# A new order for a fused sparse-attention and quick-GELU kernel: which engine adds, masks and copies from the tenth ff tile on

## The chip, the cores and the metric

The kernel runs on one core of a Trainium2 chip. Its time is the device time of one execution in microseconds; several runs are taken and their median is compared. The engines of the core are TensorE (PE in the profile, its weight loads PEld), VectorE (DVE), ScalarE (ACT), GpSimd (POOL) and SyncE (SP); transfers are issued from the queues of POOL and SP.

## What is computed

The reference first computes attention, then a feed-forward layer on its output:

```python
def _attn_ref(q, k, v):                      # (4, 8, 768, 64) each
    k_sum = k.reshape(B, H, nb, block, D).max(axis=3)      # block 32
    v_sum = v.reshape(B, H, nb, block, D).mean(axis=3)
    scores_l = scale * np.matmul(q, k.transpose(0, 1, 3, 2))
    mask_l = np.abs(pos[:, None] - pos[None, :]) < window  # window 16
    scores_s = scale * np.einsum('bhsd,bhnd->bhsn', q, k_sum) + np.log(block)
    a = softmax(concatenate([where(mask_l, scores_l, -1e9), scores_s]))
    return np.matmul(a, np.concatenate([v, v_sum], axis=2))

def _moe_ref(x, w_in, w_out):                # x (3072, 512), w_in (512, 2048)
    h = x @ w_in
    g = h * (1.0 / (1.0 + np.exp(-1.702 * h)))
    return g @ w_out                         # (3072, 512)
```

Each query thus sees 31 near keys and 24 block sums.

## The kernel before

The work runs batch by batch (0 to 3), and within a batch in three parts that are interleaved with those of the next batch. **Attention**: keys and queries of a batch are loaded by `pool.dma_start` (tiles `kb`, `qb`; values `vw`), turned (`kx`, `qT`; for batches 2 and 3 by transposing transfers on SP's queue), scored on TensorE in 64-row tiles (`ps_s`), exponentiated on ScalarE (`a_sb`), multiplied with a 0/1 mask `mk`, and multiplied with the values (`ps_av`). **ff**: `x @ w_in` for 16 tiles of 128 hidden units and two halves of 384 tokens, into PSUM tile `ph`; each tile is 4 matmuls of 128x384, and ScalarE writes its GELU to `gT`. **Products**: `g @ w_out` in a scheme with 7 instead of 8 block products (a Strassen-Winograd step), which needs sums and differences of quarters of `gT` (tile `gs`) and of `w_out` (tile `ws`); three groups of 128 tokens have seven products each (8 matmuls of 128x256 into `poA`, `poB`, `poC`), which are copied or added out of PSUM (`s`, `osb`) and stored.

Nothing is scheduled at run time: every instruction stands in a table of words, `ORDER`, that is played from the first to the last, and each engine runs its instructions in that order:

```python
    engines = {"d": dve, "a": act, "g": pool}
    for word in ORDER.split():
        name, *args = word.split(".")
        ops[name](*[engines[a] if a in engines else ... for a in args])
```

An engine therefore never passes an instruction that waits. The words that the change and the prediction speak of:

- `f.half.tile.k0123.bank`: one ff tile; `g.half.tile`: its GELU (ACT).
- `gs.j.n.what.engine`: one quarter sum over `n` hidden tiles (128x768 for n = 2, 128x384 for n = 1), VectorE if no engine is named. Sum 0 is the right half's two quarters added, 1 is sum 0 less a left quarter, 2 a difference of left and right, 3 the last one less sum 1.
- `p.t.what.bank`: product `what` of token group `t`; product 5 needs sums 0, product 6 sums 1, product 7 sums 2, product 3 sums 3, of all eight hidden tiles. `x.t.what.engine`: its copy or addition out of PSUM; `o`: the store.
- `s.b.half.pair.bank`, `e`, `m`, `v`, `nn`: scores, exponentials, mask product, values and normalisation. `vm` and `vb`: block sums of values.
- `lk`, `lq`, `lv`: loads on POOL's queue. `xk`, `xq`: transposing transfers on SP's queue. `xa`: block maxima of the transposed keys (DVE, `ka`); `ka`: copies of halo columns within `kx`; `kR`: the maxima written into `kx`; scores of the batch need all of these.
- `sd`, `ha`: small transfers within `vw` on SP's queue.

The helper that records every instruction is line 28, so all groups of the profile carry L28.

Of the kernel before, what the change touches and what calls it, by code (L numbers as in the profile page):

```python
# [49 lines left out]
f.1.0.k01.2 f.1.8.k23 ha.1.3.0 f.1.9.k0123.0 f.1.0.k23 ws.1.1 g.1.8 g.1.9 f.1.1.k0123.1 ws.2.0 f.1.2.k0123.3 g.1.0  # L50
f.1.3.k0123.2 g.1.1 ws.1.0 gs.0.2.0 ha.1.2.0 f.1.10.k0123.1 g.1.3 gs.0.2.1 f.1.4.k0123.2 g.1.2 gs.2.2.2 g.1.10 lv.1.5.0
gs.0.2.3 f.1.11.k0123.1 g.1.4 f.1.12.k0123.3 g.1.11 f.1.13.k0123.0 ws.3.1 tk.0.52 g.1.13 gs.2.2.0 g.1.12 kc.0.a
f.1.6.k0123.2 gs.0.2.2 gs.2.2.1 f.1.15.k0123.0 f.1.5.k0123.1 ws.3.0 g.1.6 g.1.5 tk.1.52 kc.1.a tk.2.42 kh.0.1.d ws.2.1
f.1.14.k0123.3 f.1.7.k0123.1 tk.3.52 gs.2.2.3 kc.2.a xm.0.1 tq.0.42 gs.4.2.0 g.1.15 kc.3.d p.0.2.0 g.1.7 g.1.14 gs.6.1.0
p.0.1.2 qc.0.a xm.1.1 tq.1.52 ha.1.1.0 gs.4.2.2 lq.2.0 x.0.1.a gs.4.2.1 gs.6.1.2 lq.2.2 gs.6.1.1 gs.7.1.0 ha.1.0.0
qc.1.a gs.6.1.3 lv.2.0.0 tq.2.42 p.1.1.3 qc.2.a gs.7.1.1 gs.4.2.3 p.0.5.1 x.0.5.a p.0.6 tq.3.52 kr.0.1.d s.1.0.0.42
x.0.6.a x.0.2.a gs.7.1.2 X gs.7.1.3 kr.1.1.d x.1.1.d xm.3.1 kh.2.1.g p.1.2.0 e.0.0 p.0.3 p.0.7 lq.2.3 m.0.0 x.0.3.a
x.0.7.a kh.1.1.d qc.3.d s.1.1.0.42 e.1.0 p.1.6 xm.2.1 vm.1.42 o.0.0.0.0.2 s.1.0.1.52 lv.2.5.0 e.0.1 kr.2.1.g kh.3.1.d
p.0.4 vb sd.1.1.0 x.0.4.a gate.1 s.1.1.1.52 e.1.1 lv.2.3.0 p.1.5.1 kr.3.1.d x.1.5.d x.1.2.a m.1.0 x.1.6.a s.1.0.2.52
# [904 lines left out]
```

## Time and profile before

| what | value |
| --- | --- |
| median of 3 runs | 212.17 us (210.46 to 212.53) |
| the profiled execution | 211.7 us, of which the span of the core is 210.0 us |
| mean granted clock of TensorE | 0.996 |
| busy: PE, DVE, ACT, POOL | 200.4, 130.8, 114.3, 109.1 us |
| instructions: DVE, ACT, POOL | 311, 227, 157 |
| loaded and stored | 27.26 MB read, 6.29 MB written |

The times of an engine are sums of its instructions' durations; an instruction that has begun but is held up counts as busy. Idle time of an engine that nothing waits for costs nothing, so the table says which engine is full, and not yet which wait is paid for.

### The profile page before, as it was taken

To read this page: it belongs to the slowest core of one execution; us is meant where nothing else is said; L and a number is where in the kernel's file an instruction comes from. 1 tells how busy PE (TensorE), PEld (TensorE's weight loads), DVE (VectorE), ACT (ScalarE), POOL (GpSimd) and SP (SyncE) were. 2 spreads that over 40 slices of the span, in tenths; PEclk is the share of its full clock that TensorE was granted. 3 is DMA by queue.
4 is the path that set the end of the run, shared out by engine and by line. 5 is a ranking of instruction groups with operands and counts; after the bars stand their busy time and mean duration, and the time that the engine had idled before them with its cause. 6 is when DMAs were issued, how large, how long until landed. Compare 5 with 4: busy or idle time off the path is not lost.

```text
span 210.0 us, 5880 instructions
## 1 busy us (share of the span) xinstructions
PE 200.4 (95%) x2440; PEld 145.8 (69%) x2440; DVE 130.8 (62%) x311; ACT 114.3 (54%) x227; POOL 109.1 (52%) x157
## 2 busy tenths in 40 slices
PE   7998798999999999999999999999999999999993
PEld 5656554667887886556788865657888865668882
DVE  5577873798997871168997822694888500166342
ACT  2473885659666736676764336567670157671100
POOL 7999972399982998448949422431000000863000
PEclk9999999999999999999999999999999999999998
DMA  4999999999999999999999999939215920000214
GB/s 67 162 166 189 209 213 221 182 144 122 99 134 199 156 177 183 130 126 141 148 166 204 142 227 180 187 29 169 50 53 139 160 105 0 0 3 0 100 53 150
DMA packets 96458, 27.74 MB, mean 132 GB/s; under 512 B 85024, under 2 KB 93488, under 8 KB 96432
## 3 DMA queue, kind: packets, MB, share of 16 engines
q0 software_dynamic: 70800, 13.64, 82.7%
q1 hardware_dynamic: 25632, 13.74, 33.2%
q8 instruction: 19, 0.31, 0.6%
q14 instruction: 7, 0.06, 0.1%
HBM read 27.26 MB, written 6.29 MB: 160 GB/s over the span
## 4 chain that ended last, share of the span: by engine, by line
PE 79%; POOL 12%; DMA 5%; issue 1%; DVE 1%; SPq 0%; POOLq 0%; DVEq 0%
PE ph L28 36%; PE poA L28 19%; PE poB L28 10%; PE poC L28 5%; PE ps_s L28 3%; PE ps_av L28 3%; DMA vw<-vw 2%; POOL mk L28 2%; DMA out_dram<-osb 2%; POOL v0n L28 2%; POOL w_in_sb L28 2%; POOL kb L28 2%; POOL kx L28 2%; POOL qb L28 1%; PE ps_t L28 1%
## 5 line engine op out<-in xcount | busy, mean ns | idle before, releaser
L28 PE MATMUL ph<-xT,w_in_sb 128*128 128x384 f16 x512 | 86.1, 326 | 0.4 <-DVE osb L28 0.4
L28 ACT ACTIVATE gT<-ph 128x384 f16<-128x384 f32 x128 | 56.1, 495 | 30.6 <-PE ph L28 29.9
L28 PEld LDWEIGHTS <-w_in_sb 128*128 128x128 f16 x512 | 49.2, 98 | 32.4 <-issue 0.9
L28 PEld LDWEIGHTS <-gs 128*128 128x128 f16 x384 | 36.5, 98 | 4.6
L28 DVE TENSOR_TENSOR gs<-gT 128x768 f16<-128x768 f16 (+1 forms) x36 | 17.5, 498 | 29.1 <-ACT gT L28 29.0
L28 POOL TENSOR_TENSOR gs<-gs,gT 128x768 f16<-128x768 f16 (+1 forms) x6 | 8.8, 1461 | 41.8 <-PE ph L28 32.7
L28 POOL DMA_DIRECT2D kb<-in_k_dram x28 | 23.1, 842 | 13.7 <-DMA w_out_sb<-in_moe_w_out_dram 6.4
L28 ACT ACTIVATE a_sb<-ps_s 128x768 bf16<-128x768 f32 x32 | 24.8, 808 | 9.5 <-PE ps_s L28 9.3
L28 PEld LDWEIGHTS <-gT 128*128 128x128 f16 x288 | 27.3, 98 | 3.6
L28 POOL DMA_DIRECT2D vw<-in_v_dram x36 | 25.7, 752 | 5.0 <-DMA w_out_sb<-in_moe_w_out_dram 1.7
L28 PE MATMUL poA<-ws,gs 128*128 128x256 f16 x192 | 24.8, 273 | 0.0
L28 POOL DMA_DIRECT2D qb<-in_q_dram x28 | 23.8, 867 | 1.8 <-issue 0.9
L28 DVE TENSOR_TENSOR a_sb<-a_sb,mk 128x768 bf16<-128x768 bf16 x28 | 14.7, 550 | 3.0 <-ACT a_sb L28 2.2
L28 DVE TENSOR_TENSOR x<-ps_av,rc 128x768 f16<-128x768 f32 (+1 forms) x18 | 15.6, 869 | 0.6
L28 ACT ACTIVATE s<-poA 128x256 f32<-128x256 f32 x14 | 5.4, 382 | 19.3 <-PE poA L28 18.6
L28 PE MATMUL poB<-ws,gs 128*128 128x256 f16 x96 | 12.5, 273 | 0.0
L28 PE MATMUL poC<-w_out_sb,gT 128*128 128x256 f16 x96 | 12.5, 273 | 0.0
L28 PE MATMUL poA<-w_out_sb,gT 128*128 128x256 f16 x96 | 12.4, 273 | 0.0
L28 PE MATMUL poB<-w_out_sb,gs 128*128 128x256 f16 x96 | 12.4, 273 | 0.0
L28 PE MATMUL poA<-ws,gT 128*128 128x256 f16 x96 | 12.3, 273 | 0.0
L28 DVE TENSOR_REDUCE ka<-kx 128x48 bf16<-128x1536 bf16 x4 | 7.0, 1750 | 7.4 <-DMA kx<-kb 7.4
...
(102 smaller groups left out, 219.0 us busy)
## 6 DMA issues: line engine op xcount, KB each, us to landing
...
```

The lines of the kernel that those rows point to most:

```text
L28: r = f(*a, **kw)
```

## The change

The first 180 words of `ORDER` stay. From there on, from the tenth ff tile of batch 0, all 822 words stand in another order; they are the same operations, and 46 of them name another engine:

- 10 more quarter sums are on GpSimd (21 where there were 11), and 5 mask products of the 32 are, where there was none.
- The halo copies `ka` of batch 2 go from GpSimd to VectorE, those of batch 3 from VectorE to GpSimd; one small `kr` copy goes to GpSimd.
- Copies out of PSUM are exchanged between VectorE and ScalarE, so that VectorE has 7 fewer and ScalarE 6 more instructions.

Two functions take the engine as an argument:

```diff
@@ ORDER, from word 181 on
-lk.1.5 lk.1.6 lq.1.2 lk.1.7 m.1.1 lq.1.1 lv.1.0.0 lq.1.4 lq.1.5 lq.1.7 lv.1.3.1 lq.1.6 lv.1.0.1 lv.1.2.0 lv.1.1.0 cv.1
+lk.1.5 lk.1.6 lq.1.2 lk.1.7 m.1.1 lq.1.1 lv.1.0.0 lq.1.4 cv.1 lq.1.5 lq.1.7 lv.1.3.1 f.0.8.k0123.2 lq.1.6 lv.1.0.1
...
@@ mask
-    def mask(half, p):
+    def mask(half, p, eng=dve):
         a = a_sb[half, p]
-        dve.tensor_mul(a, a, mk[:, half * TH:(half + 1) * TH, :].unsqueeze(1)
+        eng.tensor_mul(a, a, mk[:, half * TH:(half + 1) * TH, :].unsqueeze(1)
                        .to_broadcast([128, 2, TH, QT]))
@@ w_sum
-    def w_sum(what, part):
+    def w_sum(what, part, eng=dve):
...
-        dve.tensor_tensor(out=ws[:, what, c], in0=a, in1=b, op=ALU.subtract)
+        eng.tensor_tensor(out=ws[:, what, c], in0=a, in1=b, op=ALU.subtract)
```

No `ws` word names an engine, so those sums stay on VectorE.

Three places show what the table does to the queues. The first is GpSimd's queue in the ff part of batch 1. Before (`qb`, `kb` and `vw` are loads for the next batches, `kx` the halo copies):

```order
L28 DMA vw_106<-in_v_dram 64x8x64 x2
L28 DMA qb<-in_q_dram 128x6x64
L28 DMA vw_106<-in_v_dram 64x8x64
L28 DMA qb<-in_q_dram 128x6x64 x2
L28 DMA vw_107<-in_v_dram 64x8x64
L28 DMA kb<-in_k_dram 128x6x64
L28 TENSOR_TENSOR gs<-gs,gT 128x768
L28 DMA kb<-in_k_dram 128x6x64
L28 DMA vw_107<-in_v_dram 64x8x64
L28 COPY kx_102<-kx_102 128x4x5x16 x2
L28 COPY kx_102<-kx_102 128x24x2x16
```

and changed:

```order
L28 DMA vw_106<-in_v_dram 64x8x64
L28 TENSOR_TENSOR gs<-gT 128x768
L28 TENSOR_TENSOR gs<-gs,gT 128x768
L28 DMA qb<-in_q_dram 128x6x64
L28 TENSOR_TENSOR gs<-gs,gT 128x768
L28 DMA qb<-in_q_dram 128x6x64
L28 TENSOR_TENSOR gs<-gT,gs 128x768
L28 DMA vw_107<-in_v_dram 64x8x64
L28 DMA kb<-in_k_dram 128x6x64 x2
L28 TENSOR_TENSOR gs<-gT 128x384
```

The last two loads of queries of batch 2 (`lq.2.5`, `lq.2.7`) now stand behind two and three quarter sums, and the halo copies have left this queue for VectorE's.

The second is the same queue in batch 2, from the last loads of batch 3 on. Before:

```order
L28 DMA kb<-in_k_dram 128x6x64
L28 CAST gate_120<-xT_115 128x1
L28 DMA qb<-in_q_dram 128x6x64
L28 DMA vw_107<-in_v_dram 64x8x64
L28 DMA qb<-in_q_dram 128x6x64
L28 TENSOR_TENSOR gs<-gT 128x768
L28 DMA qb<-in_q_dram 128x6x64
L28 TENSOR_TENSOR gs<-gs,gT 128x768
L28 TENSOR_TENSOR gs<-gs,gT 128x384
```

and changed:

```order
L28 TENSOR_TENSOR gs<-gT 128x768
L28 DMA qb<-in_q_dram 128x6x64
L28 DMA vw_107<-in_v_dram 64x8x64 x2
L28 DMA kb<-in_k_dram 128x6x64
L28 CAST gate_120<-xT_115 128x1
L28 DMA qb<-in_q_dram 128x6x64
...
L28 TENSOR_TENSOR gs<-gs,gT 128x768
L28 COPY kx_103<-kx_103 128x4x5x16 x2
L28 COPY kx_103<-kx_103 128x24x2x16
L28 TENSOR_TENSOR gs<-gs,gT 128x768
L28 TENSOR_TENSOR gs<-gs,gT 128x384
L28 TENSOR_TENSOR gs<-gT,gs 128x768
L28 TENSOR_TENSOR a_sb<-a_sb,mk 128x768 x4
```

The quarter sum `gs.0.2.2.g`, which needs two GELUs of this batch, now stands ahead of the last load of keys for batch 3 (`lk.3.6`), and in the last seven rows GpSimd has the halo copies, four quarter sums and four mask products.

The third is VectorE's queue in the products of batch 2, from the first to the fourth copy out of PSUM. Changed:

```order
L28 COPY kx_103<-ka 128x24x24 x2
L28 TENSOR_TENSOR gs<-gT 128x384
L28 TENSOR_TENSOR gs<-gs,gT 128x384
L28 COPY s_2841<-poA 128x256
L28 TENSOR_TENSOR gs<-gT 128x768
L28 TENSOR_TENSOR osb<-poC,s_2841 128x256
L28 COPY s_2880<-poB 128x256
L28 TENSOR_TENSOR gs<-gT,gs 128x768
L28 TENSOR_TENSOR gs<-gT 128x384
L28 TENSOR_TENSOR gs<-gT,gs 128x384
L28 TENSOR_TENSOR a_sb<-a_sb,mk 128x768
```

Between the copies out of PSUM stand sums and mask products that read two SBUF tiles, as they did before; the ones that are gone from here are on GpSimd in the same part of the program.

More of the change, by code (lines that the diff above doesn't have):

```diff
@@ L45 @@
 g.0.2 g.0.0 g.0.1 g.0.4 g.0.6 g.0.3 lk.1.3 lq.1.0 g.0.7 g.0.5 lq.1.3 ck.1 m.1.0 m.1.2 ow.1 lk.1.4 lk.1.1 lk.1.2 lv.1.5.1
-lk.1.5 lk.1.6 lq.1.2 lk.1.7 m.1.1 lq.1.1 lv.1.0.0 lq.1.4 lq.1.5 lq.1.7 lv.1.3.1 lq.1.6 lv.1.0.1 lv.1.2.0 lv.1.1.0 cv.1
-lv.1.1.1 lv.1.4.0 lv.1.2.1 f.0.8.k0123.2 lv.1.4.1 late m.1.3 ws.0.0 g.0.8 f.0.9.k0123.3 f.0.11.k0123.0 g.0.9
-f.0.10.k0123.1 v.0.1.0.40 v.0.1.1.41 lv.1.3.0 nn.1.0 g.0.11 g.0.10 v.0.1.2.50 f.0.13.k0123.3 f.0.12.k0123.2 t.1.0.42
-v.0.1.3.51 nn.1.1 f.0.15.k0123.0 g.0.12 f.0.14.k0123.1 g.0.13 t.1.1.52 c.1.0.d c.1.1.d g.0.15 ws.0.1 g.0.14 f.1.8.k01.3
@@ L50 @@
[L50 to L59, printed above, removed]
@@ new lines @@
+lv.1.2.0 lv.1.1.0 lv.1.1.1 lv.1.4.0 lv.1.2.1 lv.1.4.1 late f.0.11.k0123.0 m.1.3 ws.0.0 f.0.10.k0123.1 f.0.9.k0123.3
+g.0.11 v.0.1.0.40 v.0.1.1.41 nn.1.0 g.0.9 v.0.1.2.50 v.0.1.3.51 f.0.13.k0123.3 f.0.15.k0123.0 t.1.0.42 g.0.8
+f.0.12.k0123.2 nn.1.1 c.1.0.d t.1.1.52 g.0.13 g.0.10 c.1.1.d g.0.12 ws.2.0 f.0.14.k0123.1 ws.1.0 f.1.8.k01.3 g.0.14
+ws.2.1 f.1.0.k01.2 g.0.15 f.1.0.k23 g.1.0 f.1.8.k23 g.1.8 f.1.1.k0123.1 g.1.1 f.1.9.k0123.0 f.1.3.k0123.2 ws.0.1
+f.1.10.k0123.1 g.1.9 g.1.3 g.1.10 gs.0.2.0 f.1.13.k0123.0 f.1.2.k0123.3 ws.3.0 g.1.13 g.1.2 f.1.11.k0123.1 f.1.4.k0123.2
@@ new lines @@
+f.1.12.k0123.3 g.1.11 f.1.15.k0123.0 ws.1.1 tk.0.52 g.1.4 f.1.5.k0123.1 g.1.12 gs.2.2.2 lv.1.3.0 kc.0.a g.1.5
+f.1.6.k0123.2 gs.2.2.0 ws.3.1 f.1.14.k0123.3 gs.0.2.2 g.1.15 gs.0.2.1 g.1.6 tk.1.52 kc.1.a tk.2.42 f.1.7.k0123.1 xm.0.1
+tk.3.52 p.0.1.2 gs.6.1.2 gs.2.2.1 gs.4.2.0 g.1.14 lv.1.5.0 gs.0.2.3 kh.1.1.d g.1.7 gs.4.2.2 kc.2.a gs.4.2.1 gs.7.1.0
+gs.6.1.0 p.1.1.3 kh.0.1.d kc.3.a tq.0.42 xm.3.1 p.0.2.0 qc.0.d X ha.1.2.0 gs.7.1.1 x.0.1.d tq.1.52 x.0.2.a lq.2.0 qc.1.a
+gs.6.1.1 kr.3.1.g gs.4.2.3 p.0.5.1 kr.0.1.d gs.7.1.2.g gs.2.2.3 tq.2.42 gs.7.1.3 qc.2.a p.0.6 xm.1.1 x.0.5.a p.1.2.0
@@ new lines @@
+lq.2.2 s.1.0.0.42 tq.3.52 gs.6.1.3 e.0.0 x.0.6.a kr.1.1.d kh.3.1.d p.0.3 qc.3.a x.1.1.d x.0.3.a o.0.0.0.0.2 s.1.1.0.42
+s.1.0.1.52 lv.2.0.0 p.0.7 e.1.0 vm.1.42 xm.2.1 lq.2.3 kr.2.1.g ha.1.3.0 m.0.0.g e.0.1 vb p.1.5.1 kh.2.1.g sd.1.1.0
+x.0.7.a lv.2.5.0 p.1.6 ha.1.0.0 sd.1.0.0 x.1.5.a s.1.1.1.52 e.1.1 s.1.0.3.42 x.1.6.d p.1.3 p.1.7 m.0.1 x.1.2.a gate.1
+e.0.3 p.0.4 s.1.1.3.42 lv.2.3.0 x.0.4.a x.1.7.a lv.2.1.1 s.1.0.2.52 p.1.4 x.1.3.a lk.2.0 e.0.2 e.1.3 lk.2.2 s.1.1.2.52
+e.1.2 lv.2.2.0 m.1.1 p.2.1.2 p.2.5.1 lv.2.2.1 lk.2.3 m.1.3 m.1.0 m.0.2 x.1.4.a ha.1.1.0 v.1.1.0.40 v.1.0.0.50 v.1.1.1.41
@@ new lines @@
+v.1.0.1.51 lv.2.5.1 G p.2.2.3 lk.2.1 x.2.5.a lk.2.4 p.2.3 o.0.1.0.0.2 nn.1.0 x.2.1.a lk.2.5 lk.2.7 p.2.6 nn.0.0 lk.2.6
+t.1.0.42 m.0.3 lv.2.1.0 lq.2.1 o.0.0.1.0.2 t.0.0.52 m.1.2 x.2.6.a lv.2.0.1 c.0.0.d o.0.1.1.0.2 c.1.0.a p.2.7 x.2.2.a
+x.2.7.a v.1.0.2.50 v.1.0.3.51 nn.0.1 v.1.1.2.40 x.2.3.a v.1.1.3.41 p.2.4 lq.2.4 x.2.4.a t.0.1.52 xk.0.0.1 c.0.1.d
+f.0.9.k01.3 f.0.8.k01.1 f.0.0.k01.2 f.0.0.k23 f.0.1.k01.0 g.0.0 nn.1.1 f.0.9.k23 g.0.9 lv.2.3.1 t.1.1.42 c.1.1.d
+xk.0.1.0 f.0.1.k23 f.0.8.k23 f.1.0.k0123.2 g.0.8 f.1.9.k0123.3 o.0.2.1.0.2 f.1.8.k0123.1 g.0.1 g.1.0 g.1.9 g.1.8
@@ new lines @@
+f.1.1.k0123.0 f.1.10.k0123.3 g.1.1 f.0.2.k0123.2 g.1.10 xk.0.0.0 lv.2.4.0 g.0.2 f.0.10.k0123.0 f.1.2.k0123.1 g.1.2
+f.0.3.k0123.2 xk.0.1.1 g.0.10 f.1.11.k0123.3 f.1.3.k0123.1 g.0.3 lq.2.6 f.0.4.k0123.2 lv.2.4.1 g.1.11 f.1.12.k0123.3
+g.1.3 f.0.11.k0123.0 gs.2.2.0 f.1.4.k0123.1 g.0.4 g.1.12 g.0.11 g.1.4 f.0.5.k0123.2 gs.0.2.0.g gs.0.2.2.d gs.0.2.1.g
+f.1.15.k0123.3 xq.0.0 g.0.5 lq.2.5 ha.2.0.0 g.1.15 f.1.5.k0123.1 f.0.6.k0123.2 g.0.6 f.0.12.k0123.0 f.1.13.k0123.3 g.1.5
+f.1.6.k0123.1 g.0.12 g.1.13 f.1.7.k0123.2 xa.0.0 gs.2.2.1.g ka.0.d g.1.7 g.1.6 f.0.13.k0123.0 lq.2.7 xq.0.1 g.0.13
@@ new lines @@
+gs.2.2.3.g lv.3.1.0 xa.1.0 vm.2.42 f.1.14.k0123.3 f.0.14.k0123.0 f.0.7.k0123.1 lk.3.0 g.1.14 g.0.14 g.0.7 gs.6.1.0
+kR.0.d gs.6.1.2.d lk.3.4 gs.7.1.0.g gs.4.2.0 vb p.0.1.2 gs.6.1.1 f.0.15.k0123.0 g.0.15 o.0.2.0.0.2 gs.4.2.1 gs.4.2.2.d
+gs.7.1.1 ha.2.2.0 sd.2.1.0 lv.3.1.1 gs.7.1.2 X x.0.1.d p.2.5.1 s.2.0.1.52 sd.2.0.0 s.2.0.0.42 p.0.2.0 lk.3.2 e.0.1
+p.0.5.3 lk.3.7 e.0.0 p.0.6 gs.0.2.3.g gs.7.1.3.g x.0.2.a x.0.5.d gs.4.2.3 lk.3.3 x.0.6.a s.2.0.2.42 lk.3.5 ha.2.3.0
+gs.2.2.2.d gs.6.1.3 s.2.0.3.52 p.0.3 p.1.5.0 m.0.1 e.0.3 e.0.2 s.2.1.1.52 s.2.1.0.42 m.0.3 p.0.7 e.1.1 e.1.0 lv.3.4.1
@@ new lines @@
+m.0.0 lv.3.0.1 x.0.3.a p.1.1.3 ha.2.1.0 s.2.1.3.52 x.0.7.a e.1.3 x.1.5.a x.1.1.d s.2.1.2.42 lv.3.5.0 e.1.2 o.1.0.0.0.2
+p.0.4 p.1.6 v.2.0.0.40 x.0.4.a m.0.2 x.1.6.a v.2.0.2.50 lv.3.2.0 lk.3.1 v.2.0.1.41 o.1.0.1.0.2 v.2.0.3.51 m.1.3 p.1.2.2
+m.1.2 p.1.3 nn.0.0 m.1.0 x.1.2.a nn.0.1 p.1.7 lv.3.3.0 lq.3.0 p.2.1.2 G x.1.3.a d.0.0 v.2.1.0.40 x.2.1.a m.1.1
+v.2.1.2.50 x.1.7.a v.2.1.1.41 v.2.1.3.51 p.2.6 x.2.5.a o.1.1.0.0.2 lq.3.4 x.2.6.a nn.1.0 p.1.4 nn.1.1 p.2.7 x.1.4.a
+d.0.1 p.2.3 lv.3.0.0 x.2.7.a p.2.2.3 x.2.2.a p.2.4 d.1.0 f.0.1.k01.0 x.2.3.a d.1.1 lq.3.5 f.0.8.k01.1 x.2.4.d
@@ new lines @@
+f.0.9.k01.3 xk.1.0.0 f.0.0.k01.2 f.0.0.k23 g.0.0 f.0.8.k23 f.0.1.k23 f.0.9.k23 g.0.1 g.0.8 f.1.0.k0123.2 g.0.9
+f.1.1.k0123.0 g.1.0 lv.3.3.1 lq.3.7 f.1.8.k0123.1 g.1.1 g.1.8 f.0.2.k0123.2 gs.0.2.2.g f.1.9.k0123.3 g.0.2 f.1.2.k0123.1
+g.1.9 lq.3.3 lv.3.4.0 g.1.2 f.0.10.k0123.0 lv.3.2.1 f.1.10.k0123.3 xk.1.0.1 f.1.3.k0123.1 g.1.10 f.0.3.k0123.2
+f.1.11.k0123.3 g.0.10 lk.3.6 g.1.3 gate.2 xa.0.1 lq.3.6 lv.3.5.1 lq.3.1 g.1.11 o.1.1.1.0.2 f.1.5.k0123.1 gs.2.2.0 lq.3.2
+g.0.3 f.0.11.k0123.0 gs.2.2.1.g g.1.5 gs.2.2.2.d xk.1.1.1 f.1.12.k0123.3 f.0.4.k0123.2 g.0.11 xk.1.1.0 g.1.12 gs.2.2.3.g
@@ new lines @@
+g.0.4 f.0.12.k0123.1 f.0.13.k0123.0 f.0.7.k0123.2 xq.1.0 xq.1.1 ha.3.3.0 f.1.14.k0123.3 g.0.12 g.0.13 f.1.4.k0123.0
+g.0.7 g.1.14 g.1.4 f.1.6.k0123.1 f.0.5.k0123.2 gs.0.2.0.d f.0.14.k0123.0 o.1.2.1.0.2 vm.3.52 f.1.13.k0123.3 g.1.6
+f.1.7.k0123.1 ha.3.1.0 g.0.5 f.0.6.k0123.2 vb g.0.14 g.1.13 gs.6.1.0 gs.4.2.0 xa.1.1 f.1.15.k0123.3 o.1.2.0.0.2
+f.0.15.k0123.0 g.0.6 kR.1.d g.1.7 sd.3.0.0 p.0.1.2 g.0.15 gs.0.2.1.g g.1.15 ka.1.g p.1.2.0 gs.7.1.0 gs.6.1.1 s.3.0.1.42
+x.0.1.d s.3.0.0.52 p.0.2.3 gs.4.2.2 p.0.5.1 x.0.2.a X e.0.0 x.0.5.d gs.4.2.1.g e.0.1 ha.3.2.0 s.3.0.2.52 gs.0.2.3
@@ new lines @@
+gs.7.1.2 gs.7.1.1.g s.3.0.3.42 e.0.2 p.1.1.3 gs.6.1.3 m.0.1 p.0.6 e.0.3 s.3.1.0.52 x.0.6.a gs.4.2.3.g gs.6.1.2
+s.3.1.1.42 sd.3.1.0 x.1.1.a gs.7.1.3 e.1.1 p.0.3 m.0.2 e.1.0 p.0.7 x.0.3.a s.3.1.2.52 s.3.1.3.42 x.0.7.a m.1.0.g p.1.6
+e.1.3 p.1.5.1 p.0.4 x.1.6.a m.0.3.g e.1.2 x.0.4.a p.1.7 x.1.2.a ha.3.0.0 m.0.0 v.3.0.0.50 x.1.5.d o.2.0.0.0.2 v.3.0.2.40
+o.2.0.1.0.2 m.1.1 v.3.0.3.41 v.3.0.1.51 x.1.7.a m.1.3.g nn.0.0 nn.0.1 p.1.4 x.1.4.a G p.1.3 m.1.2.g x.1.3.a d.0.0
+p.2.1.2 x.2.1.a p.2.2.3 x.2.2.a v.3.1.2.40 v.3.1.3.41 v.3.1.0.50 v.3.1.1.51 d.0.1 p.2.6 p.2.5.1 nn.1.0 nn.1.1 x.2.6.a
@@ new lines @@
+o.2.1.0.0.2 x.2.5.d p.2.7 x.2.7.a d.1.0 f.0.9.k01.3 f.0.1.k01.0 p.2.3 p.2.4 x.2.3.a x.2.4.d f.0.1.k23 g.0.1 d.1.1
+f.0.8.k01.1 f.0.9.k23 f.0.8.k23 f.0.0.k01.2 g.0.8 f.0.0.k23 g.0.9 f.1.1.k0123.0 f.1.9.k0123.3 f.1.8.k0123.1 g.1.1
+o.2.2.1.0.2 g.0.0 f.1.0.k0123.2 g.1.8 f.0.10.k0123.0 g.1.9 f.1.11.k0123.3 o.2.2.0.0.2 f.1.2.k0123.1 g.1.0 g.0.10 g.1.11
+f.0.2.k0123.2 f.1.13.k0123.3 f.0.11.k0123.0 g.0.2 g.1.13 g.1.2 f.0.3.k0123.2 f.1.3.k0123.1 f.1.10.k0123.3 g.0.3 g.1.3
+g.1.10 f.0.4.k0123.2 f.1.4.k0123.1 g.0.4 g.0.11 gs.0.2.0.g f.1.12.k0123.3 g.1.4 gs.0.2.2.d f.0.5.k0123.2 g.0.5 g.1.12
@@ new lines @@
+f.0.12.k0123.0 f.1.5.k0123.1 gs.2.2.0.d g.1.5 f.1.14.k0123.3 gs.2.2.2.d f.0.6.k0123.2 g.0.12 f.1.6.k0123.1 g.0.6 g.1.6
+gs.2.2.1.g gs.4.2.2.d gs.0.2.1.g f.0.13.k0123.0 g.0.13 f.0.7.k0123.2 f.1.7.k0123.1 g.1.14 g.0.7 g.1.7 gs.2.2.3.g
+f.1.15.k0123.3 gs.0.2.3.g gs.4.2.0.d gs.6.1.0.d P7.0 o.2.1.1.0.2 f.0.15.k0123.0 gs.6.1.1 g.0.15 g.1.15 p.0.1.2 gs.7.1.0
+gs.6.1.2.g x.0.1.a f.0.14.k0123.0 p.0.5.1 gs.4.2.1 gs.7.1.1.d g.0.14 p.0.6 gs.6.1.3 p.1.1.3 x.0.6.a p.0.2.0 gs.4.2.3
+gs.7.1.2 p.0.7 gs.7.1.3.d x.0.5.a x.0.2.a x.0.7.a x.1.1.a p.0.3 p.0.4 x.0.3.a p.1.5.1 x.0.4.a p.1.6 x.1.6.d p.1.2.2
@@ L110 @@
+x.1.5.d x.1.2.a o.3.0.0.0.2 p.1.7 x.1.7.a o.3.0.1.0.2 p.2.1.2 p.1.3 x.1.3.a x.2.1.a p.2.6 x.2.6.d o.3.1.0.0.2 p.2.5.1
+p.2.7 p.2.2.0 x.2.5.d p.2.3 x.2.2.a p.1.4 x.1.4.a x.2.7.a p.2.4 o.3.2.1.1.2 x.2.4.a x.2.3.a o.3.2.0.0.2 o.3.1.1.0.2
+o.3.2.1.0.1
 """
```

50 lines of the change are left out of this document (removed).

## The prediction

> **What bounds the kernel now.** I read the page's busy line first, then the busy time by stage, then TensorE's idle time in the timeline.
>
> ```profile
> PE 200.4 (95%) x2440; PEld 145.8 (69%) x2440; DVE 130.8 (62%) x311; ACT 114.3 (54%) x227; POOL 109.1 (52%) x157
> core 0: us, PE busy (x) PEld busy (x) DVE busy (x) ACT busy (x) POOL busy (x), PEclk, DMA share, GB/s
> 34.69:77.30 42.61, 42.61 (x608) 32.41 (x609) 34.97 (x82) 26.96 (x49) 32.84 (x47) 1.00 1.69 152
> 77.30:99.40 22.10, 22.10 (x190) 13.57 (x189) 10.85 (x17) 14.11 (x32) 14.88 (x19) 1.00 2.03 152
> 99.40:122.70 23.30, 22.86 (x361) 19.29 (x360) 19.31 (x46) 11.56 (x20) 14.75 (x20) 1.00 1.84 171
> 122.70:144.60 21.90, 21.50 (x176) 12.80 (x175) 12.78 (x25) 13.61 (x32) 6.70 (x7) 1.00 0.94 148
> 144.60:167.10 22.50, 22.50 (x361) 19.34 (x361) 17.09 (x39) 10.69 (x17) 0.91 (x1) 1.00 0.51 109
> ...
> 100.79 0.66 PE L28 MATMUL ps_s<-qT,kx 64*128 64x64 bf16 x24 [0.43 <-issue]
> 123.10 8.12 PE L28 MATMUL ph<-xT,w_in_sb 128*128 128x384 f16 x49 [0.41 <-DVE osb L28]
> ```
>
> From 34.69 us on, PE fills every stage but two, which lack 0.44 and 0.40 us. The last two rows name these gaps: the scores of batch 2 (0.43), which come after VectorE's `kR.0.d`, and the first ff tile of batch 2 (0.41) behind an output addition. The granted clock is 1.00. All that stands before 34.69 lies within the unchanged words or ends with their last transfer, and all matmuls remain. So the change can remove 0.84 us of idling, and otherwise only add it. DVE and POOL are busy for 17.1 and 0.9 us of 22.5 in the products of batch 2: the room the change fills on POOL.
>
> **The change part by part.** Prices come from the groups by form, and the runs of 64-row groups from the chain.
>
> ```profile
> L28 DVE TENSOR_TENSOR gs<-gT 128x768 f16<-128x768 f16 x20 | 11.9, 610 | 22.4 <-ACT gT L28 22.3
> L28 POOL TENSOR_TENSOR gs<-gs,gT 128x768 f16<-128x768 f16 x4 | 6.9, 1734 | 35.8 <-PE ph L28 32.7 <-DVE gs L28 3.1
> L28 DVE TENSOR_TENSOR a_sb<-a_sb,mk 128x768 bf16<-128x768 bf16 x28 | 14.7, 550 | 3.0 <-ACT a_sb L28 2.2 <-POOL mk L28 0.7
> L28 POOL COPY kx<-kx 128x768 bf16<-128x768 bf16 x1 | 1.1, 1147 | 0.0
> L28 ACT ACTIVATE s<-poA 128x256 f32<-128x256 f32 x14 | 5.4, 382 | 19.3 <-PE poA L28 18.6 <-DMA qb<-in_q_dram 0.7
> 63.48 0.98 PE poB L28 x8
> 65.72 0.87 PE poB L28 x8
> ```
>
> A 128x768 sum costs 0.55 to 0.61 us on DVE and 1.73 on POOL. Eight more such sums, two of half the width and five masks add about 8 x 1.7 + 2 x 0.9 + 5 x 1.65 = 24 us to POOL. A mask on POOL is not in the trace: from below 1.15 (the one-input copy of that shape), from above 1.73; I take 1.65, as it reads two tiles like the sums. DVE is rid of some 13 x 0.55 + 2 x 0.35 = 7.9 us and seven copies. Six more copies on ACT are 6 x 0.38 = 2.3 us, in its 19.3 us of waiting for those products: 0. If that cover were gone, a product would wait 0.4 for its bank. *Entries into 64-row groups*: a product behind one takes 0.98 instead of 0.87. The new order has 23 such runs instead of 26: 3 x 0.11 = **-0.3**.
>
> What a POOL sum does to DVE stands in the timeline:
>
> ```profile
> 90.75 1.75 DVE L28 TENSOR_REDUCE ka<-kx 128x48 bf16<-128x1536 bf16 x1 [5.92 <-DMA kx<-kb]
> 92.06 1.65 POOL L28 TENSOR_TENSOR gs<-gs,gT 128x768 f16<-128x768 f16 x1
> 92.42 1.71 DVE L28 TENSOR_TENSOR gs<-gT 128x768 f16<-128x768 f16 x1
> 139.66 2.10 DVE L28 COPY kx<-kx 128x320 bf16<-128x320 bf16 x3
> 139.84 1.71 POOL L28 TENSOR_TENSOR gs<-gs,gT 128x768 f16<-128x768 f16 x1 [3.12 <-DVE gs L28]
> 185.61 1.76 POOL L28 TENSOR_TENSOR gs<-gs,gT 128x768 f16<-128x768 f16 x1
> 185.79 2.26 DVE L28 TENSOR_TENSOR gs<-gs,gT 128x768 f16<-128x768 f16 x2
> ```
>
> The reduction beside POOL's sum takes what it always takes. The DVE sum at 92.42 takes 1.71 instead of 0.55 and ends 0.42 after POOL's: held for 1.16. At 139.66 three copies take 2.10; the two small ones are through in about 0.4, the wide one is held until POOL ends (about 1.2 more than the 0.5 it should need). At 185.79 two sums take 2.26 instead of 1.10: 1.16 again. So three of before's eight wide POOL sums held DVE, each for about 1.2. With 13 wide operations more this is 13 x 3/8 x 1.2 = 5.9 us of DVE time, most of the 7.9 it is rid of. *The Trainium skill, "SBUF — State Buffer", section "Who interferes with whom", says that a DVE instruction with two SBUF inputs and a GpSimd instruction that reads SBUF exclude each other for a whole instruction, and that the reduction never contends; the rows agree. By that rule every overlap would hold DVE, 13 x 1.2 = 15.6 us instead of 5.9, a loss; that is the first rival below.*
>
> *Batch 0*, the transfers within `vw` before `v.1.1.0`:
>
> ```profile
> 62.83 1.18 DVE L28 TENSOR_TENSOR vs<-ps_vs,vpart 32x128 bf16<-32x128 f32 x4
> 64.04 1.24 SPq L28 DMA_DIRECT2D vw<-vs  x2
> DMA to landing us min/median/max: 2.9/4.2/5.0
> 70.30 0.95 PE L28 MATMUL ps_av<-vw,a_sb 128*64 128x65 bf16 x48
> ```
>
> Before, the halo transfers `ha` had gone ahead of the two that wait for `vb` (64.04). Now `ha.1.0.0` and `ha.1.1.0` stand on SP behind `sd.1.1.0` and `sd.1.0.0`. At 0.62 each, the fourth is issued at 65.9 and lands 2.9 to 5.0 later, at 68.8 to 70.9. The values need it at 70.3, with 16 products ahead of them as before: from 1.5 to spare to 0.6 late, and to 1.2 if `vb` comes one product later. Behind it waits nothing but PE itself. I take **+0.4** (0 to 1.2). The mask `m.0.0` on POOL ends ten us before its use: 0.
>
> *Batch 1*, the maxima and sums before the first products:
>
> ```profile
> 78.41 8.40 SPq L28 DMA_TRANSPOSE kx<-kb  x4
> DMA to landing us min/median/max: 8.1/10.1/10.7
> DMA to landing us min/median/max: 10.6/10.8/11.0
> 100.13 0.77 DVE L28 COPY kx<-ka 128x576 bf16<-128x576 bf16 x2
> 99.32 1.04 PE L28 MATMUL poC<-w_out_sb,gT 128*128 128x256 f16 x8
> ```
>
> The second row is for the four transposing transfers, the third for `lq.2.5` and `lq.2.7` (issued 83.8 and 84.6). The second half of the first key tile now goes third, some 0.3 us late for a store between, and lands near 78.4 + 2 x 2.1 + 10.1 + 0.3 = 93.0, where the maxima of that tile began at 90.75. Then DVE has maxima 1.75, halo copies 0.9 (2.10 if held), maxima 1.75, a sum 0.35, `kR` 0.77, two sums 0.9: to 99.4 or 100.6. The second product, which needs these sums, is due at 99.32 + 0.87 = 100.2. So the wait of 0.43 goes or stays; but the next late one is the additions of `vb` (1.5) and six sums and copies (about 2.9) up to `x.0.1.d`, at 103.8 without a hold, before `p.0.6`, due at 100.2 + 0.9 (the second product) + 0.6 (two score groups) + 2 x 0.9 = 103.5. Late by 0.3, with two holds by 2.7. Two POOL sums lie beside it: 2 x 3/8 x 1.2 = 0.9, less a little that falls on DVE's waits for PE. **+1.0** (0.3 to 2.7). The loads behind POOL's three sums are issued 3 to 5 us later; since those rows took 10.6 to 11.0 to land, when the queue was backlogged, I expect them to land less than 1 us later: 0 (bounds 0 and 3; `xq.0.1` waits for them).
>
> *Batch 2*, the last keys of batch 3:
>
> ```profile
> 116.74 0.89 POOL L28 DMA_DIRECT2D kb<-in_k_dram  x1
> DMA to landing us min/median/max: 5.1/5.1/5.1
> 128.74 2.92 SPq L28 DMA_TRANSPOSE kx<-kb  x2
> DMA to landing us min/median/max: 3.7/4.1/4.8
> 136.96 1.75 DVE L28 TENSOR_REDUCE ka<-kx 128x48 bf16<-128x1536 bf16 x1
> 138.75 0.53 DVE L28 COPY kx<-ka 128x576 bf16<-128x576 bf16 x2
> 144.63 0.52 PE L28 MATMUL ps_s<-qT,kx 64*128 64x64 bf16 x24
> ```
>
> `lk.3.6` left at 116.74. Now `gs.0.2.2.g` is ahead of it and waits for the GELU of the sixth ff tile: 123.1 + 6 x 0.66 (four matmuls each, 8.12 us for 49) + 0.5 = 127.6; the sum ends at 129.3, three loads at 0.8 go first, issue 131.6, 15 us later. It lands 5.1 later as it did (the second row), at 136.7; the second of the pair of transposing transfers goes 1.5 after the first and lands 3.7 to 4.8 later (the fourth row, all four of this tile): 141.9 to 143.0. Maxima and `kR` make 144.2 to 145.3, and the halo copies, now on POOL for 2.2, 144.1 to 145.2. The scores have two products ahead of them now, so they are due at 144.63 + 1.75 = 146.4: in time by 1.1 to 2.2. Landings as in batch 1 (8.1 to 10.7) would make it 2 to 5 late, but the DMA share here is 0.94 against 2.03. Behind the halo copies POOL has `gs.4.2.1.g` (1.7), `gs.7.1.1.g` (0.9) and `gs.4.2.3.g` (1.7): to 148.4 to 149.5, or 1.7 sooner for `p.0.6`, which is due at 146.4 + 1.1 + 3 x 0.9 = 150.2; `p.0.3` comes 1.5 later. DVE's sums for the same products run beside them, held once or twice by 1.2, with about 1 to spare: one hold leaves 0.2 over, two 1.4. **+0.4** (0, and 3.8 by the first rival). The four late masks end about 2 us before their values: 0.
>
> *Batch 3*: POOL has six sums where it had seven, in other places; a hold of 1.2 may fall on the last before `p.0.5.1`: **+0.1** (0 to 1.2).
>
> *The two waits*: **-0.84**. Should one stay, this is -0.4.
>
> Sum: -0.3 - 0.84 + 0.4 + 1.0 + 0.4 + 0.1 = **+0.8**. The profiled execution took 211.7 (span 210.0, 1.7 around it), so 212.5; it lies 0.5 below the median of 212.17, so against that **212.9 us**.
>
> **The rivals.** (1) *POOL's operations hold DVE at the end of batch 2* (slower). It decides once the last key transfer lands 1 us later than 143.0: then the sums on both engines run side by side. Four holds (three POOL sums and the first mask) are 4 x 1.2 = 4.8, less 1.0 to spare, in place of the 0.4: 212.9 + 3.4 = 216.3. For it: every row of a hold above. Against: DVE has less to do there, and the transfers in that stage were quiet. (2) *Loads and transfers late in batches 0 and 1* (slower): all upper ends there, +0.8 and +1.7: 215.4. For it: SP and POOL play their queues in order, and the DMA share is highest there (2.03). Against: the same backlog hides a later issue. (3) *All waits go and none comes* (faster): 212.17 - 1.14 = 211.0. For it: DVE and ACT have room in every place. Against: three places above are within 1 us of their due times. (4) *The change does nothing*, as DVE was off the path nearly everywhere: 212.2, inside the forecast.
>
> **How the numbers follow.** Forecast: 0.58, of which (4) has 0.15. Rivals: (1) 0.12, (2) 0.16, (3) 0.14. A measurement of this kernel tells about 1% (2.1 us) from no change. Faster by more would need 210.0, beyond the 211.0 of rival 3; by the runs' own spread (210.46 to 212.53) 0.04. Slower by more is over 214.3: rivals 1 and 2, and 0.03 of the forecast: 0.31. Within: 0.65. The range goes from 210.8 (rival 3 less a little spread) to 216.3; the forecast's own is 211.2 to 214.3.
>
> **What would show it.** PE's idling after 34.69 should be 1 to 3 us in place of 0.84, in the timeline before `ps_av` of batch 0 (on `vw`), before `poA` or `poB` near 103 (on DVE), and little before `ps_s` near 146. POOL should be busy for some 130 us, DVE for about 125, with more DVE sums of 1.7. It is wrong if PE idles over 3 us in one place (rivals 1, 2), or if matmuls themselves take longer.

## The result, and the profile after

The changed kernel takes 213.1 us (median of 20 runs, 211.88 to 215.19), the kernel before 211.58 (20 runs, 210.39 to 214.01): a ratio of 1.0067, 95% interval 1.004 to 1.0094. Ratios are of means, without the executions that took over 1.5% more than the fastest of their kernel (here those of 215.19 and 214.01 us). The prediction was 212.9, within 1% of the kernel before. The changed kernel's profiled execution took 212.19, its span 210.5.

The page's busy line, TensorE's stages, and the two largest waits of the changed kernel (the windows go from the values at the end of the lead-in to the last product of each batch; columns as in the prediction):

```profile
PE 200.2 (95%) x2440; PEld 145.2 (69%) x2440; DVE 128.3 (61%) x289; ACT 118.6 (56%) x233; POOL 134.7 (64%) x173
34.54:76.66 42.12, 41.75 (x608) 32.01 (x601) 35.37 (x80) 27.16 (x50) 35.76 (x50) 1.00 1.67 157
76.66:124.10 47.44, 45.35 (x549) 32.70 (x550) 30.03 (x58) 27.21 (x53) 33.91 (x38) 1.00 1.66 155
124.10:168.75 44.65, 44.65 (x542) 32.55 (x540) 26.65 (x48) 25.99 (x51) 26.21 (x23) 1.00 0.81 124
168.75:207.24 38.49, 38.49 (x293) 28.38 (x290) 14.61 (x28) 16.99 (x39) 10.31 (x6) 1.00 0.14 48
101.70 0.61 PE L28 MATMUL poB<-ws,gs 128*128 128x256 f16 x4 [1.45 <-DVE gs L28]
103.12 0.35 PE L28 MATMUL ps_s<-qT,kx 64*128 64x64 bf16 x12 [0.52 <-DVE vs L28]
```

POOL is 25.6 us busier (24 worked out); DVE only 2.5 us less (some 6 forecast), with 22 instructions fewer. TensorE idles 0.37 us in batch 0 and 2.09 in batch 1, and not at all in batches 2 and 3. The 2.09 us are one event, late sums on VectorE. The timeline of VectorE and GpSimd just ahead of it:

```profile
97.29 1.67 POOL L28 DMA_DIRECT2D kb<-in_k_dram  x2
97.56 1.47 DVE L28 TENSOR_TENSOR gs<-gT 128x384 f16<-128x384 f16 x1 [2.53 <-ACT gT L28]
98.95 1.96 DVE L28 COPY kx<-ka 128x576 bf16<-128x576 bf16 x2
98.96 1.78 POOL L28 TENSOR_TENSOR gs<-gT,gs 128x768 f16<-128x768 f16 x1
100.83 0.82 DVE L28 TENSOR_TENSOR gs<-gT 128x384 f16<-128x384 f16 x2
101.57 0.28 DVE L28 COPY vpart<-ps_vs 128x128 f32<-128x128 f32 x1
```

The second row is `gs.6.1.0`, a sum that takes 0.35 us elsewhere: it takes 1.47. The third is `kR.0.d`, 0.53 in batch 2 of before: it takes 1.96, its second copy being held until POOL's sum `gs.0.2.3.g` (fourth row, ends 100.74) is through. Together 1.12 + 1.44 = 2.56 us, of which the product and the scores behind them wait 1.45 + 0.52. The first hold is new: beside `gs.6.1.0` there is no GpSimd sum, only the issue of two loads, `lk.3.2` and `lk.3.7`. Such issues did not hold VectorE in the profile of before:

```profile
98.92 2.46 POOL L28 DMA_DIRECT2D kb<-in_k_dram  x3
99.87 0.34 DVE L28 TENSOR_TENSOR gs<-gT 128x384 f16<-128x384 f16 x1
```

What differs is what stands behind the loads in GpSimd's queue: in the changed kernel a sum whose inputs have long been there. That gives **theory A**: a GpSimd sum that is ready holds VectorE's two-input sums already while GpSimd still issues the loads ahead of it. **Theory B**: the new order makes this chain late, whichever engine adds. **Theory C**: the issue of these loads holds VectorE by itself.

### The profile page after: what moved, and what is told of

The parts are those of the page before. It is cut to its first block, busy times and chain, and to the rows that moved or that the text cites. A ratio compares the mean times of both kernels' runs of the same rounds, so it can differ in the third digit from the quotient of the medians.

```text
span 210.5 us, 5886 instructions
## 1 busy us (share of the span) xinstructions
PE 200.2 (95%) x2440; PEld 145.2 (69%) x2440; DVE 128.3 (61%) x289; ACT 118.6 (56%) x233; POOL 134.7 (64%) x173
## 5 line engine op out<-in xcount | busy, mean ns | idle before, releaser
L28 ACT ACTIVATE gT<-ph 128x384 f16<-128x384 f32 x128 | 58.2, 491 | 34.7 <-PE ph L28 34.0
L28 DVE TENSOR_TENSOR gs<-gT 128x768 f16<-128x768 f16 (+1 forms) x34 | 22.1, 671 | 27.8 <-ACT gT L28 27.8
L28 POOL TENSOR_TENSOR gs<-gT 128x384 f16<-128x384 f16 (+1 forms) x6 | 8.1, 1355 | 25.8 <-ACT gT L28 25.6
L28 POOL TENSOR_TENSOR gs<-gs,gT 128x768 f16<-128x768 f16 (+1 forms) x8 | 12.9, 1622 | 7.6 <-DVE gs L28 7.6
L28 DVE TENSOR_TENSOR x<-ps_av,rc 128x768 f16<-128x768 f32 (+1 forms) x18 | 15.6, 869 | 0.6
L28 ACT ACTIVATE s<-poA 128x256 f32<-128x256 f32 x16 | 6.0, 382 | 17.6 <-PE poA L28 16.0
L28 POOL TENSOR_TENSOR gs<-gT,gs 128x768 f16<-128x768 f16 (+1 forms) x7 | 12.0, 1720 | 4.2 <-DVE gs L28 4.1
L28 ACT ACTIVATE osb<-poA 128x256 f32<-128x256 f32 x10 | 3.9, 388 | 15.1 <-PE poA L28 15.1
```

Of the source, the lines that this page charges most:

```text
L28: r = f(*a, **kw)
```

## The experiments

**One sum back on VectorE** (and, at another place, two loads moved behind a sum):

```diff
-gs.0.2.3.g            # batch 1
+gs.0.2.3
-lv.3.5.1 lq.3.1 ... lq.3.2 ... gs.2.2.1.g      # batch 2
+lv.3.5.1 ... gs.2.2.1.g lq.3.1 lq.3.2
```

> The changed kernel, with the sum gs.0.2.3 of batch 1 back on VectorE (GpSimd then has only loads and a sum that is not yet ready at 97 to 104 us), and in batch 2 the loads lq.3.1 and lq.3.2 behind gs.2.2.1.g instead of ahead of it. Theory A (a GpSimd sum that is ready and queued behind load issues holds VectorE from then on): gs.6.1.0 takes 0.35 instead of 1.47, the two kR copies 0.6 instead of 1.96, the waits of 1.45 and 0.52 us before the second product and the scores of batch 2 go below 0.3 together, and the time falls by 1.5 to 2.0 us, to some 211.3. Theory C (the load issues themselves hold VectorE): gs.6.1.0 still takes about 1.4, only the kR copies become short, a wait of about 0.3 stays. Theory B (the new order makes the chain late, whoever does the sum): both waits stay, 213. In batch 2, gs.0.2.0.d took 3.30 us beside two load issues and a sum; by A it takes up to 1.8, held by the sum alone, by C 0.55 or 1.8.

Measured 210.8 us (10 runs; ratio to before 0.9951, 0.992 to 0.9981). The same place in the timeline:

```profile
99.05 1.68 POOL L28 DMA_DIRECT2D kb<-in_k_dram  x2
99.32 0.36 DVE L28 TENSOR_TENSOR gs<-gT 128x384 f16<-128x384 f16 x1 [2.68 <-ACT gT L28]
99.59 0.65 DVE L28 COPY kx<-ka 128x576 bf16<-128x576 bf16 x2
```

The same sum beside the same two loads now takes 0.36, the copies 0.65, and both waits are gone. C is out for the sum, and B for these waits. (For the copies a little of C is true: see the last section.) The time is that of both edits, so it prices neither alone. The other place tells the same. In batch 2 VectorE has three sums in a row, 0.56, 0.55 and then `gs.0.2.0.d`; the groups of three, first in the changed kernel, then here:

```profile
134.41 4.25 DVE L28 TENSOR_TENSOR gs<-gT 128x768 f16<-128x768 f16 x3 [3.73 <-ACT gT L28]
134.88 1.69 POOL L28 DMA_DIRECT2D qb<-in_q_dram  x2
136.53 1.70 POOL L28 TENSOR_TENSOR gs<-gs,gT 128x768 f16<-128x768 f16 x1
```

```profile
134.28 2.94 DVE L28 TENSOR_TENSOR gs<-gT 128x768 f16<-128x768 f16 x3 [3.77 <-ACT gT L28]
135.02 1.79 POOL L28 TENSOR_TENSOR gs<-gs,gT 128x768 f16<-128x768 f16 x1 [0.22 <-ACT gT L28]
136.76 1.70 POOL L28 DMA_DIRECT2D qb<-in_q_dram  x2
```

With the loads ahead of GpSimd's sum the third takes 3.30 us: it begins at 135.35, after the first of the three has written GpSimd's input (134.97), and gets through only when loads and sum are done. With the loads behind the sum it takes 2.00, somewhat more than the 1.8 that was the upper end.

**The sum earlier on GpSimd.** The same sum, moved ahead in GpSimd's queue, VectorE's work unchanged:

```diff
-gs.2.2.3.g lv.3.1.0 xa.1.0 ... lk.3.2 ... lk.3.7 ... p.0.6 gs.0.2.3.g gs.7.1.3.g
+gs.2.2.3.g gs.0.2.3.g lv.3.1.0 xa.1.0 ... lk.3.2 ... lk.3.7 ... p.0.6 gs.7.1.3.g
```

> The changed kernel, with gs.0.2.3.g of batch 1 moved ahead in GpSimd's queue, directly behind gs.2.2.3.g; VectorE's work is the same. Theory A: the holds of gs.6.1.0 and kR go, the waits of 1.45 and 0.52 us with them, idling of TensorE after the lead-in 0.4 to 0.9 instead of 2.46, time 211.0 to 211.6, level with or below the kernel before. Theory C: the loads behind it are 1.7 us later and still lie beside gs.6.1.0 or kR, which stay held; a wait of 0.5 to 1.5. Theory B: as the changed kernel, 213.

Measured 209.72 us (6 runs, 209.36 to 210.26; ratio 0.9896, 0.9864 to 0.9928): below both kernels.

```profile
76.32:121.50 45.18, 45.07 (x550) 32.75 (x551) 29.43 (x58) 26.99 (x53) 33.68 (x38) 1.00 1.69 161
90.85 3.24 POOL L28 TENSOR_TENSOR gs<-gT,gs 128x768 f16<-128x768 f16 x2
91.27 3.35 DVE L28 COPY kx<-kx 128x320 bf16<-128x320 bf16 x3
98.20 1.67 POOL L28 DMA_DIRECT2D kb<-in_k_dram  x2
98.24 0.81 DVE L28 TENSOR_TENSOR gs<-gT 128x384 f16<-128x384 f16 x2
```

Batch 1 idles 0.11 us instead of 2.09. The halo copies at 91.27 are held for 2.6 us (for some 0.9 in the changed kernel, where the three took 1.68), but there nothing waits for them; and beside the same loads (98.20) VectorE is free. So it is not the amount of holding that costs.

**The order alone.** The changed table, with 30 words of sums, masks and `kx` copies on their old engines:

```diff
-... gs.0.2.0.g ... gs.2.2.1.g ka.0.d ... m.1.0.g ...
+... gs.0.2.0 ... gs.2.2.1 ka.0.g ... m.1.0 ...
```

> The new order with every quarter sum, mask product and kx copy on the engine that it had before (30 words changed back); the exchange of output copies between VectorE and ScalarE stays. If GpSimd's holds are the loss (A), TensorE idles less than 1 us after the lead-in and the time is 211 to 211.8. If the order is the loss (B), the waits before the second product and the scores of batch 2 stay at 1.5 to 2 us and the time is near 213.

Measured 213.81 us (7 runs; ratio 1.0086, 1.0045 to 1.0127). Neither side is confirmed: the waits of the hold are gone, and others have come, the largest on transfers.

```profile
105.43 0.53 PE L28 MATMUL ps_s<-qT,kx 64*128 64x64 bf16 x24 [0.62 <-DMA qT<-qb]
113.41 0.79 PE L28 MATMUL ps_av<-vw,a_sb 128*64 128x65 bf16 x37 [0.79 <-DMA vw<-vw]
148.00 0.52 PE L28 MATMUL ps_s<-qT,kx 64*128 64x64 bf16 x24 [0.64 <-DMA vw<-vs]
```

**The engines alone.** The order of before, with those 30 words on their new engines:

```diff
-... gs.0.2.0 ... ka.0.g ... gs.2.2.1 ... gs.2.2.3 ...
+... gs.0.2.0.g ... ka.0.d ... gs.2.2.1.g ... gs.2.2.3.g ...
```

> The order of before, with the quarter sums, mask products and kx copies on the engines that the change names (30 words). A: the sums now on GpSimd hold VectorE wherever they fall, in places that nobody chose; 1 to 4 us more idling than before, 213 to 215. B: as before, 211.6.

Measured 233.03 us (4 runs; ratio 1.0948, 1.0881 to 1.1015), far outside both. The largest wait is no hold:

```profile
140.32 2.00 POOL L28 TENSOR_TENSOR gs<-gT 128x768 f16<-128x768 f16 x1 [5.24 <-ACT gT L28]
144.73 0.70 POOL L28 DMA_DIRECT2D vw<-in_v_dram  x1
148.25 0.31 PE L28 MATMUL ps_vs<-vw,E 64*32 64x128 bf16 x7 [5.85 <-DMA vw<-in_v_dram]
```

A sum that waits 5.24 us for GELUs stands ahead of a load of values, and TensorE waits 5.85 us for that load. (The profiled execution also had a granted clock of 0.954, so not all of the 21 us are waits.) Order and engines of this change belong together; neither can be priced without the other.

**The hold put into the kernel before.**

```diff
-lk.3.7 ... lk.3.3 gs.2.2.1 ... gs.2.2.3 lk.3.5
+lk.3.7 ... gs.2.2.1 ... gs.2.2.3.g lk.3.3 lk.3.5
```

> The kernel before with one sum moved: gs.2.2.3 of batch 1 from VectorE to GpSimd, behind the loads lk.3.2 and lk.3.7 (its inputs are ready before these loads are issued), and lk.3.3 behind it. VectorE is rid of 0.55 us, its chain towards the scores of batch 2 starts earlier. If only the sum's own run matters (C, or no hold at all), kR.0.d ends near 99.8 instead of 100.9, the wait of 0.43 us before these scores goes, and the time is the same or 0.4 less. If a ready sum behind loads holds VectorE from the loads on (A), gs.7.1.0 or kR stretches by 1 to 3 us beside lk.3.2, lk.3.7 and the sum, the scores wait 0.5 to 2.5 us, and the time is 0.3 to 2 us more than before.

```profile
98.79 1.69 DVE L28 TENSOR_TENSOR gs<-gT 128x384 f16<-128x384 f16 x1
99.23 1.64 POOL L28 DMA_DIRECT2D kb<-in_k_dram  x2
100.40 2.31 DVE L28 COPY kx<-ka 128x576 bf16<-128x576 bf16 x2
100.88 1.65 POOL L28 TENSOR_TENSOR gs<-gT,gs 128x768 f16<-128x768 f16 x1
101.12 0.21 PE L28 MATMUL ps_s<-qT,kx 64*128 64x64 bf16 x2 [0.72 <-DVE kx L28]
102.77 0.49 PE L28 MATMUL ps_s<-qT,kx 64*128 64x64 bf16 x22 [1.44 <-DVE kx L28]
```

The profile shows what A asks for: both stretches, and 2.16 us of waiting. (At its start `gs.7.1.0` also lies beside the last GpSimd copy, until 99.30.) Yet the median is 211.77 (10 runs, 210.66 to 215.1; ratio 0.9985, 0.9942 to 1.0027), level with before. A was right on the event and wrong on the time. The profiles further down say why the time does not show it: the kernel before has waits of its own of that size in two of its three profiles.

**The late masks back on VectorE**, in the kernel with the sum earlier:

```diff
-m.1.0.g ... m.0.3.g ... m.1.3.g ... m.1.2.g
+m.1.0 ... m.0.3 ... m.1.3 ... m.1.2
```

> The kernel with gs.0.2.3.g moved ahead (209.7), with the four mask products at the end of batch 2 (m.1.0, m.0.3, m.1.3, m.1.2 of batch 3) back on VectorE. If masks on GpSimd are free, as predicted (they end before their use, and TensorE shows no wait there), TensorE's busy time and idling in that stage stay, and the time is 209.4 to 210.0. If they had relieved VectorE where it is full, waits of 0.3 to 1 us come before the values or products of that stage.

Measured 210.1 us (10 runs; ratio 0.9936, 0.99 to 0.9972), and batches 2 and 3 take 44.65 and 38.49 us, to the hundredth as with the masks on GpSimd. They cost nothing and gain nothing.

**A copy back on VectorE**, in the same kernel, batch 0:

```diff
-p.1.6 ... x.1.5.a s.1.1.1.52
+p.1.6 ... x.1.5.d s.1.1.1.52
```

> The kernel with gs.0.2.3.g moved ahead (209.7), with one output copy of batch 0 (x.1.5) back from ScalarE to VectorE. The wait of 0.26 us before p.1.3 (poB, behind ScalarE's copy) goes: 0.26 less idling, 209.4. It is also a near copy of that kernel: if its 2.2 us under the kernel before were a chance of the time up to the first 34 us, this one falls back towards 210.8 (before less 0.5 of idling and 0.5 of the stages); if not, it stays at 209.4 to 209.8.

Measured 210.3 us (12 runs; ratio 0.9927, 0.9896 to 0.9959). The wait did not go; it changed its name. In the first two rows, of the changed kernel, ScalarE's copy itself waits, for the addition `osb<-poA,s` that VectorE makes behind the additions of `vb`: it reads the buffer that the copy is to write. On VectorE (last row) the copy comes behind the same addition.

```profile
62.86 0.38 ACT L28 ACTIVATE s<-poB 128x256 f32<-128x256 f32 x1 [2.45 <-DVE osb L28]
63.30 1.03 PE L28 MATMUL poB<-w_out_sb,gs 128*128 128x256 f16 x8 [0.26 <-ACT s L28]
...
64.63 1.03 PE L28 MATMUL poB<-w_out_sb,gs 128*128 128x256 f16 x8 [0.29 <-DVE s L28]
```

As a near copy it puts the earlier kernel's 209.7 in its place: about 210, 0.7 to 1.0% below before, part of the first figure probably being a short lead-in (33.6 us there, 34.8 in its second profile, 35.8 here).

**The changed kernel again.**

> The changed kernel itself, on the same chip as the three others: 212.9 to 213.3, and its waits before the second product and the scores of batch 2 (1.45 and 0.52 us) again within 0.3 of that, since the holds follow from the order of the queues and not from chance. If they were chance (transfers landing late once), they differ by more than 0.5.

Measured 212.7 us (10 runs; ratio 1.005, 1.0003 to 1.0097). That is just under the range, and the two waits are 1.46 and 0.52, where its first profile had 1.45 and 0.52. The hold came back with the order of the queues:

```profile
97.22 1.48 DVE L28 TENSOR_TENSOR gs<-gT 128x384 f16<-128x384 f16 x1 [2.39 <-ACT gT L28]
101.38 0.61 PE L28 MATMUL poB<-ws,gs 128*128 128x256 f16 x4 [1.46 <-DVE gs L28]
102.80 0.35 PE L28 MATMUL ps_s<-qT,kx 64*128 64x64 bf16 x12 [0.52 <-DVE vs L28]
```

**More profiles of single executions.** The kernel before twice, the kernel with the sum earlier and the one with the hold once each:

> The kernel before, profiled once more. Its times spread over 4 us (210.4 to 215.1) at a full clock, and the kernel with one moved sum, which has 1.2 us more in its stages, measured level with it. If the first profile of before is typical, the time from the last values of the lead-in to the last product is again 171.3 to 171.8 us with 0.6 to 1.1 us of idling, and the spread lies in the lead-in (33.6 to 36). If before has a wait that varies, it shows here or in the next look: idling of 1.5 to 4 us, most likely before the scores of batch 2, behind key transfers.

> As the look before it: 171.3 to 171.8 us between lead-in and last product if the first profile is typical, more if a wait varies.

> The kernel with gs.0.2.3.g moved ahead, profiled once more: 170.5 to 171.1 us from the lead-in to the last product and 0.4 to 0.9 us of idling, as before in its first profile (171.0, 0.68); the lead-in may differ by 2 us.

> The kernel before with gs.2.2.3 on GpSimd behind two loads, profiled once more. If the hold follows from the queues, gs.7.1.0 and the second kR copy are stretched by over 1 us each again and the scores wait about 2 us (172.5 to 173). If it depends on when key transfers land, one of them is short and the wait below 1.2 us.

The time from the end of the lead-in to the last product in each profile:

| kernel | total us | TensorE busy | idle |
| --- | --- | --- | --- |
| before, three profiles | 171.5, 173.0, 172.8 | 170.7, 170.8, 170.9 | 0.8, 2.2, 1.9 |
| changed, two profiles | 172.7, 172.8 | 170.2, 170.2 | 2.5, 2.6 |
| sum earlier, two profiles | 171.0, 170.6 | 170.3, 170.0 | 0.7, 0.6 |
| hold in before, two profiles | 172.7, 171.7 | 170.5, 170.7 | 2.2, 1.0 |

The first profile of before was its best; it was not typical. The two others wait longer, at other places, most of it on transfers; the columns are total, times, longest:

```profile
PE ps_av L28 <- DMA vw<-vw: 1.6, 2, 0.9
...
PE ph L28 <- DVE osb L28: 0.6, 1, 0.6
```

```profile
PE ph L28 <- DVE osb L28: 1.6, 1, 1.6
```

The first fence is the second profile (0.63 of the 1.6 falls before the end of the lead-in), the other the third. The ff tile waits for an output addition that waited 2.37 us for a store: `osb` comes free when the store lands.

In the second profile of the hold GpSimd reached its sum 2.6 us earlier (98.31 instead of 100.88), and ahead of `gs.7.1.0`:

```profile
98.31 1.66 POOL L28 TENSOR_TENSOR gs<-gT,gs 128x768 f16<-128x768 f16 x1
98.73 1.46 DVE L28 TENSOR_TENSOR gs<-gT 128x384 f16<-128x384 f16 x1
100.11 0.81 DVE L28 COPY kx<-ka 128x576 bf16<-128x576 bf16 x2
```

So `gs.7.1.0` was held by the sum's own run and not from the loads on, the `kR` copies hardly at all, and the wait was 0.76 instead of 2.16. Of the two outcomes expected it is the second: how long a hold lasts depends on when the two engines meet, and in this kernel the order of the queues does not fix that.

## Why the prediction was right

**The bound** was right for the stages behind the lead-in: TensorE has the same matmuls, and what differs there is its waits and half a microsecond of its busy time. **The entries into 64-row groups** (-0.3): TensorE's busy time between the marks is 0.5 to 0.6 us lower (170.2 against 170.7 to 170.9). That the entries make all of it was not tried.

**The two waits** (-0.84) do go, but that term was too small. It came from one profile of a kernel whose waits change from run to run; over three profiles before idles 1.6 us on average, and none of these waits shows in the two profiles of the changed kernel or the two with the sum earlier. That is a gain of 1.6 in place of 0.84. (It needs the new engines too: the order alone waits 0.79 us for `vw` again.)

**Batch 0** (+0.4): 0.37, the right size at the wrong place. The halo transfer went out at 64.47 instead of 65.9 and was in time; 0.26 of the wait is at `p.1.3`, for the copy that frees its bank, which is late because of an addition on VectorE. So the size was luck.

**Batch 1** (+1.0, at most 2.7): 2.09. The place was right, VectorE's chain ahead of the first products, and so was the cause, GpSimd's holds. The step that failed is the count: I took two sums that hold in 3 of 8 cases, by their own run alone. I did not see that a ready sum behind loads can hold from the loads on, which is 1.12 of the 2.56 us here. Nor was it `p.0.6` that waited but the second product, for the same chain. The key transfers, which I made late by 2.3 us, were not: VectorE began the maxima at 90.02, before 90.75.

**Batch 2** (+0.4) is 0, and rival 1 did not come. `lk.3.6` left at 132.42 (131.6 worked out), the halo copies were done at 143.3, `kR` at 146.9, and the scores found them ready, but by 0.35 us only, where 1.1 to 2.2 were worked out. **Batch 3** (+0.1) is 0. **The masks** were free, as said; one takes 1.63 to 1.96 us on GpSimd, near the 1.65 that I took.

**The holds in sum**: I expected 5.9 us more of VectorE's time. What each sum, mask product, wide halo copy and `kR` copy takes past its undisturbed duration adds up to 5.2 us before and 11.9 after, so 6.7 more (an estimate from one profile each); the rule that every overlap holds would have made it 15.6.

**The sum.** By the terms as they came out, 0.4 + 2.1 - 1.6 - 0.5 = +0.4 us; the stages in the profiles say +0.3 (172.8 against 172.5 on average), the ratios +1.4 (0.85 to 2.0) and, in the second comparison, +1.1 (0.1 to 2.1). So the number was partly luck: the loss in batch 1 and the gain from the old waits were each about 1 us larger than forecast, and these errors cancel. About 1 us of the measured difference is not in the stages at all. The forecast put everything outside them at no change, and no trace shows what lies there: both profiles of the changed kernel are of executions (212.19 and 211.88 us) that are 0.8 to 0.9 us faster than its medians.

One candidate is the clock. Executions of the changed kernel have a mean granted clock under 0.993 in 15 of 30 cases, and are then about 1.1 us longer than its others (213.5 against 212.3); in a profile with 0.99 the dip lies near 24 us, in the lead-in, which the change does not touch. Of the executions of before whose clock is on record, 9 of 55 have it. That would account for half a microsecond at most. Why the changed kernel should meet it more often was not tried, and the rest stays open too.

Of the rivals, the second (loads and transfers late) did not happen: where transfers are late is the kernel before. The third (all waits go) is what the kernel with the sum earlier comes near to: 0.6 to 0.7 us of idling, 209.7 to 210.3 us, against 211.0 worked out. One place in a queue stood between it and the forecast.

The 46 words in the section on the change are a balance over the whole table. Operation by operation, 54 words name another engine, since exchanges between batches cancel in that balance; the numbers of sums and masks are not affected. Of VectorE's seven instructions fewer there, six are copies out of PSUM, and the seventh is the `kr` copy.
